# The second half of a weight transposition on ACT's DMA queue, the bias rows on SP's

## The chip, the cores and the metric

The kernel runs on one core of one Trainium2 chip. A core has five engines with a queue each: TensorE (PE, matmuls; its weight loads are listed apart as PEld), VectorE (DVE), ScalarE (ACT), GpSimd (POOL) and SyncE (SP). DMAs are issued in this kernel from the queues of SP and ACT; the names SPq and ACTq in the profile are these issues. The metric is the time of one execution in microseconds on the device, the median of the runs; lower is better.

## The reference

A layer norm of x (2048 tokens of 512 values, bf16), and then two branches on the normalised xn whose outputs are added to x.

```
xn = layernorm(x)
# branch A: linear attention, 32 heads of 16
q, k, v = split(xn @ wqkv)
pq, pk  = q @ w_phi, k @ w_phi                      # per head, 16 x 16
phi(p)  = concat(softmax(p), softmax(-p))           # 32 features per head
kv, z   = sum over tokens of phi(pk)^T v, of phi(pk)
o       = (phi(pq) @ kv) / (phi(pq) @ z + 1e-6)
# branch B: a dense layer with the mish activation, F = 1792
h       = xn @ w1 + b1
act     = h * tanh(softplus(h))
out     = x + o @ wo + act @ w2
```

## The kernel before, in words

The 2048 tokens are 16 tiles of 128 (NT), in four groups of four (NG, TPG). x stays in SBUF as `x_sb`; the normalised tiles are transposed into `xnT` and serve as weights of the projections and as moving operand of the dense layer.

*Keys' weights.* The keys' projection and w_phi are folded into one matrix `wkp` on the chip: `load_turned(D, 2)` (line 161) loads the keys' 512 columns of wqkv transposed, as tile `wT`, by two DMA transpositions (line 166) of 256 rows each, into columns 0 to 255 and 256 to 511. `fold` (line 171) multiplies one 128-column strip of wT by the block-diagonal `Wbd` (made by POOL from `wsrc` and `block`). So foldk_0 and foldk_1 need the first half of wT, foldk_2 and foldk_3 the second. The queries' weights are folded the same way much later (`load_turned(0)`, one transposition of all rows), and aren't touched by the change.

*The first DMAs (lines 548 to 559).* SP issues wsrc, then the two halves of wT, then wv, x's tiles 4 to 7, the two halves of w1, and x's tiles 8 to 15. ACT issues x's tile 0, x's tiles 1 to 3, and the bias rows `b1b` (14 x 128). ACT's first arithmetic is a square root of a constant (`root`, line 564), ahead of which the table of its functions is loaded; it has that table ready by the time the first row statistics come.

*Until the first tile is there*, PE runs 11 matmuls on constants (`keep_warm`, line 586).

*The order.* Behind the first DMAs all work follows a list written out by hand, `PLAN` (line 20), which `step` (line 593) turns into instructions; each engine runs its own in this order, and waits where an operand is missing. Its beginning is

```
spread_0 block mean_0 deviate_0_1 invert_0_1 total_3 spread_2 apply_0_0 scatter_3 mean_2 flip_0
spread_1 foldk_0 deviate_2_1 foldk_1 flip=_0_1 foldk=_0_0 invert_2_1 mean_1 foldk_2 deviate_3_1
```

spread and mean are the row statistics on DVE (lines 197, 213), deviate the square root of the variance on ACT (line 218), invert its reciprocal on DVE (line 223), apply the normalisation (line 249), total and scatter the statistics of tile 3 on ACT (lines 202, 206), flip the transposition of a normalised tile on PE (line 257), flip= its copy to SBUF (line 623), foldk a fold on PE (line 174), foldk= its copy into wkp (line 627), first a part of a keys' projection (line 274), bias the transposition of b1b on PE (line 633). Later steps project values, logits and the dense layer's units, take the softmaxes, and run the second half of the attention with the second dense layer (lines 524, 533).

Of the kernel before, what the change touches and what calls it, by code (L numbers as in the profile page):

```python
# [85 lines left out]
def kernel(  # L86
# [12 lines left out]
    nc = tc.nc  # L99
# [17 lines left out]
    b1_v = B_b1.rearrange("(f p) -> f p", p=P)  # L117
# [25 lines left out]
    b1b = wts.tile([FT, P], BF16, name="b1b")  # L143
# [17 lines left out]
    def load_turned(base_col, parts=1):  # L161

        wT = lnp.tile([P, 4, 512], BF16, name="wT", tag="xn")
        n = D // parts
        for r in range(0, D, n):
            nc.sync.dma_start_transpose(
                out=wT[:, :, r : r + n], in_=A_wqkv[r : r + n, base_col : base_col + D]
            )
        return wT
# [379 lines left out]
        nc.sync.dma_start(wsrc[:], wphi_v)  # L549
    for t in (slice(0, 1), slice(1, 4)):  # L550
        nc.scalar.dma_start(x_sb[:, t, :], x_v[:, t, :])
    nc.scalar.dma_start(b1b[:], b1_v[:, :])
    held = {"wT": load_turned(D, 2)}
    nc.sync.dma_start(wv, wqkv_v[:, :, 2 * D : 3 * D])
    nc.sync.dma_start(x_sb[:, 4:8, :], x_v[:, 4:8, :])
    for c in (slice(0, F // 2), slice(F // 2, F)):
# [36 lines left out]
    def step(name):  # L593
# [53 lines left out]
        elif kind == "wo":  # L647
            nc.sync.dma_start(wo_sb, wo_v[:, :, :])
        elif kind == "wq":
            held["wT"] = load_turned(0)  # L650
        elif kind == "fold":
            held[key] = fold(held["wT"], *n)
# [87 lines left out]
```

## Time and profile before

| what | value |
|---|---|
| median of 3 runs (lowest, highest) | 174.26 us (174.21, 174.62) |
| the profiled execution's own time | 174.22 us |
| its span, first to last instruction | 172.5 us |
| PE busy | 168.5 us (98%) |
| DVE, ACT, POOL busy | 150.6, 113.0, 49.5 us |
| DMA issues on ACT's queue before its first arithmetic | x_sb twice, 0.91 us together, then b1b, 0.73 us |
| transpositions of wT on SP's queue | from 1.31 us, 3.07 us for both issues |

Times in the profile are counted from the span's first instruction, so that a run takes some 1.7 us more than its span. A row of the timeline has the start, the length, the engine, the line in the kernel, the operation and the tiles, and in brackets the idle time of the engine ahead of it with what ended it. "Landing" of a DMA is when its last part has arrived and its semaphore tells so.

### The profile page before, as it was taken

The numbers are of one execution on the slowest core, as the hardware profiler recorded it, in microseconds if no ns is written. First come the engines' busy times: TensorE is split into PE (matmuls) and PEld (weight loads), VectorE is DVE, ScalarE is ACT, GpSimd is POOL, SyncE is SP. The second block draws the span as 40 slices with busy tenths as digits, with TensorE's granted clock in tenths as the row PEclk, the third lists the DMA queues.
The fourth block names the chain that finished last, engine by engine and source line by source line (L and its number), as shares of the span: only waits on it lengthen the run. The fifth ranks groups of instructions, "written<-read, shape, count | busy, mean of one in ns | idle before, by whom it ended". The sixth has DMA issues, their size and how long they took to land.

```text
span 172.5 us, 2832 instructions
## 1 busy us (share of the span) xinstructions
PE 168.5 (98%) x1038; PEld 82.6 (48%) x1038; DVE 150.6 (87%) x265; ACT 113.0 (66%) x169; POOL 49.5 (29%) x91
## 2 busy tenths in 40 slices
PE   8999999999999999999999999999999999999993
PEld 2444444444544644455454444544544554445571
DVE  2967998999999999999999999999999899994633
ACT  4949999999999799999999998821710400400000
POOL 6003047100480005685007403341480420320000
PEclk9999999999999999999999999999999999999999
DMA  6999992647900000000000095217456556676752
GB/s 154 264 397 347 130 331 89 128 117 143 104 0 0 4 0 0 2 0 4 0 0 0 0 131 117 61 37 163 47 121 138 130 130 93 143 164 152 124 143 71
DMA packets 45226, 18.03 MB, mean 105 GB/s; under 512 B 37148, under 2 KB 45212, under 8 KB 45212
## 3 DMA queue, kind: packets, MB, share of 16 engines
q1 hardware_dynamic: 44496, 17.26, 44.5%
q10 hardware_dynamic: 716, 0.59, 1.1%
q8 instruction: 8, 0.13, 0.3%
q14 instruction: 6, 0.05, 0.1%
HBM read 6.84 MB, written 2.10 MB: 52 GB/s over the span
## 4 chain that ended last, share of the span: by engine, by line
PE 94%; DVE 2%; DMA 1%; ACT 1%; issue 0%; DVEq 0%
PE ph L289 28%; PE po L524 28%; PE pproj L274 24%; PE po L533 8%; PE pnd L488 2%; PE pkv L451 2%; DMA x_sb<-in_A_x_dram 1%; DVE stats L197 1%; PE pfold L174 1%; DVE x_sb L541 1%; PE ptr L257 1%; DVE xn L249 0%; ACT wkv L627 0%; ACT rstd L218 0%; DVE rstd L223 0%
## 5 line engine op out<-in xcount | busy, mean ns | idle before, releaser
L524 PE MATMUL po<-w_sb,acts 128*128 128x512 bf16 (+1 forms) x238 | 51.9, 366 | 0.0
L289 PE MATMUL ph<-xnT,w_sb 128*128 128x512 bf16 x224 | 50.9, 379 | 0.0
L377 ACT ACTIVATE e<-e 128x1024 bf16<-128x1024 bf16 x28 | 28.3, 1056 | 25.1 <-DVE e L347 25.0
L391 POOL TENSOR_TENSOR t<-e 128x512 f32<-128x512 bf16 x13 | 16.6, 1274 | 78.2 <-ACT e L377 78.1
L299 ACT ACTIVATE acts<-ph,b1f 128x512 bf16<-128x512 f32 x56 | 35.4, 706 | 1.2 <-PE ph L289 1.1
L289 PEld LDWEIGHTS <-w_sb 128*128 128x128 bf16 x224 | 21.5, 98 | 25.2 <-issue 0.4
L524 PEld LDWEIGHTS <-acts 128*128 128x128 bf16 x238 | 22.5, 98 | 22.9
L274 PE MATMUL pproj<-wkv,xnT 128*128 128x512 bf16 x128 | 29.4, 379 | 0.0
L274 PEld LDWEIGHTS <-xnT 128*128 128x128 bf16 x192 | 18.0, 98 | 20.1 <-ACT xnT L623 0.3
L387 DVE TENSOR_REDUCE sums<-e 128x64 f32<-128x1024 bf16 x15 | 17.9, 1212 | 1.0 <-ACT e L377 0.8
L391 POOL TENSOR_TENSOR t<-t 128x256 f32<-128x256 f32 (+1 forms) x28 | 16.1, 576 | 2.2
L533 PE MATMUL po<-wqk,ob 128*128 128x512 bf16 (+1 forms) x68 | 16.3, 366 | 0.0
L274 PE MATMUL pproj<-wqk,xnT 128*128 128x512 bf16 x64 | 15.3, 379 | 0.0
L541 DVE TENSOR_TENSOR x_sb<-po,x_sb 128x512 bf16<-128x512 f32 (+1 forms) x17 | 10.9, 650 | 4.1 <-PE po L533 4.1
L197 DVE BATCH_NORM_STATS2 stats<-x_sb 128x6 f32<-128x512 bf16 x15 | 9.4, 679 | 4.1 <-DMA x_sb<-in_A_x_dram 4.1
L504 DVE TENSOR_TENSOR ob<-pnd,r 128x512 bf16<-128x512 f32 x16 | 11.1, 691 | 0.5
L438 DVE TENSOR_TENSOR e<-e,r 128x2048 bf16<-128x2048 bf16 x8 | 9.9, 1231 | 0.3
L326 ACT CAST e<-pproj 128x512 bf16<-128x512 f32 x12 | 7.1, 605 | 4.4 <-PE pproj L274 3.9
L533 PEld LDWEIGHTS <-ob 128*128 128x128 bf16 x68 | 6.4, 98 | 6.0
L503 DVE RECIPROCAL r<-pnd 128x32 f32<-128x32 f32 x16 | 5.6, 351 | 4.0 <-PE pnd L488 3.8
L309 ACT CAST p<-pproj 128x512 bf16<-128x512 f32 x14 | 7.8, 597 | 1.6 <-PE pproj L274 1.6
L488 PEld LDWEIGHTS <-qT 128*128 128x128 bf16 x128 | 6.1, 97 | 3.9 <-issue 0.9
(80 smaller groups left out, 184.6 us busy)
## 6 DMA issues: line engine op xcount, KB each, us to landing
out_dram<-x_sb SPq DMA_DIRECT2D x15, 128.0 KB, 1.9
w_sb<-in_B_w_dram SPq DMA_DIRECT2D x2, 896.0 KB, 8.4
x_sb<-in_A_x_dram SPq DMA_DIRECT2D x3, 512.0 KB, 10.2
w_sb<-in_B_w_dram SPq DMA_DIRECT2D x2, 640.0 KB, 5.5
wkv<-in_A_wqkv_dram SPq DMA_DIRECT2D x1, 512.0 KB, 5.1
w_sb<-in_B_w_dram SPq DMA_DIRECT2D x1, 512.0 KB, 7.0
wqk<-in_A_wo_dram SPq DMA_DIRECT2D x1, 512.0 KB, 4.2
x_sb<-in_A_x_dram ACTq DMA_DIRECT2D x1, 384.0 KB, 3.2
```

The source lines that it names most:

```text
L197: nc.vector.bn_stats(statistics(t)[0][:, t % TPG, :], x_sb[:, t, :])
L274: nc.tensor.matmul(pp, lhsT=xnT[:, t, kt, :], rhs=w[:, kt, :], start=(kt == 0), stop=(kt == KT - 1),)
L289: nc.tensor.matmul(ph[:], lhsT=w1_sb[:, kt, f * P : (f + 1) * P], rhs=xnT[:, g * TPG : (g + 1) * TPG, kt, :], start=(kt == 0), stop=(kt == ...
L299: nc.scalar.activation(acts[:, f, g * 512 : (g + 1) * 512], ph[:], ACT.Mish, bias=b1f[:, f : f + 1])
L377: nc.scalar.activation(v, v, ACT.Exp)
L387: nc.vector.reduce_sum(out, part, axis=AX.X)
L391: nc.gpsimd.tensor_tensor(out=to[:], in0=part[:, :, 0:n], in1=part[:, :, n : 2 * n], op=ALU.add)
L438: nc.vector.tensor_tensor(out=vv, in0=vv, in1=r2[:, :, None, :].to_broadcast([P, 128, 8, 2]), op=ALU.mult)
L504: nc.vector.tensor_tensor(out=o_t.rearrange("p (u v g d) -> p u v g d", u=2, v=4, g=4), in0=nd[:, :, :, 0:64].rearrange("p u v (g d) -> p ...
L524: nc.tensor.matmul(po[:, c], lhsT=acts[:, f, t * P : (t + 1) * P], rhs=w2_sb[:, f, c], start=(f == 0), stop=False,)
L533: nc.tensor.matmul(po[:, c], lhsT=oT_of[h][:, 2 + t % 2, j * P : (j + 1) * P], rhs=wo_sb[:, j, c], start=False, stop=(j == 3),)
L541: nc.vector.tensor_tensor(out=y, in0=po[:, c], in1=y, op=ALU.add)
```

## The change

The second half of the keys' wT is issued on ACT's queue, where it follows x's first two loads; the first half stays on SP. The bias rows' load leaves ACT's queue and is issued by SP behind the first half of wT, ahead of wv. The rest of SP's and ACT's orders, the order on PE, DVE and POOL, and the arithmetic are the same.

```
         wT = lnp.tile([P, 4, 512], BF16, name="wT", tag="xn")
         n = D // parts
         for r in range(0, D, n):
-            nc.sync.dma_start_transpose(
+            (nc.scalar if r and parts == 2 else nc.sync).dma_start_transpose(
                 out=wT[:, :, r : r + n], in_=A_wqkv[r : r + n, base_col : base_col + D]
             )
         return wT
...
     for t in (slice(0, 1), slice(1, 4)):
         nc.scalar.dma_start(x_sb[:, t, :], x_v[:, t, :])
-    nc.scalar.dma_start(b1b[:], b1_v[:, :])
     held = {"wT": load_turned(D, 2)}
+    nc.sync.dma_start(b1b[:], b1_v[:, :])
     nc.sync.dma_start(wv, wqkv_v[:, :, 2 * D : 3 * D])
     nc.sync.dma_start(x_sb[:, 4:8, :], x_v[:, 4:8, :])
```

More of the change, by code (lines that the diff above doesn't have):

```diff
@@ L165, in load_turned @@
         for r in range(0, D, n):
-            nc.sync.dma_start_transpose(
+            (nc.scalar if r and parts == 2 else nc.sync).dma_start_transpose(
                 out=wT[:, :, r : r + n], in_=A_wqkv[r : r + n, base_col : base_col + D]
@@ L551 @@
         nc.scalar.dma_start(x_sb[:, t, :], x_v[:, t, :])
-    nc.scalar.dma_start(b1b[:], b1_v[:, :])
     held = {"wT": load_turned(D, 2)}
+    nc.sync.dma_start(b1b[:], b1_v[:, :])
     nc.sync.dma_start(wv, wqkv_v[:, :, 2 * D : 3 * D])
```

## The prediction

> **What bounds the kernel now.** I read the page first (busy shares, then the chain that ended last), then the chain in order of time over the first 9 us, and then the queues of ACT and SP row by row.
>
> ```profile
> span 172.5 us, 2832 instructions
> PE 168.5 (98%) x1038; PEld 82.6 (48%) x1038; DVE 150.6 (87%) x265; ACT 113.0 (66%) x169; POOL 49.5 (29%) x91
> PE 94%; DVE 2%; DMA 1%; ACT 1%; issue 0%; DVEq 0%
> ```
>
> The chain is TensorE for 94% of the span. The next rows are the windows (length; PE busy and its matmuls; granted clock; DMA share; GB/s).
>
> ```profile
> 5.58:8.02 2.44, 2.34 (x30) 1.00 1.01 235
> 8.02:100.00 91.98, 91.98 (x553) 1.00 0.34 87
> 100.00:168.70 68.70, 68.70 (x444) 1.00 0.59 120
> ```
>
> From 8.02 us to 168.70 PE has no idle time at all. So a start delayed by some time is an end delayed by that time; and nothing behind 8 us can give it back. What sets that start is the head of the chain (start, us, what):
>
> ```profile
> 0.79 2.29 DMA x_sb<-in_A_x_dram
> 3.11 0.70 DVE stats L197
> 3.83 0.19 DVE mv L213
> 4.05 0.30 ACT rstd L218
> 4.38 0.16 DVE rstd L223
> 4.54 0.67 DVE stats L197
> 5.21 0.33 DVE xn L249
> 5.58 0.40 PE ptr L257 x4
> ```
>
> The first x tile lands at 3.08, and ACT's square root for it (deviate_0) at 4.05 stands in the middle of the chain. Whatever keeps ACT from it moves the whole kernel.
>
> **The change, part by part.** ACT's and SP's queues before (timeline):
>
> ```profile
> 0.79 0.91 ACTq L551 DMA_DIRECT2D x_sb<-in_A_x_dram  x2
> 1.73 0.73 ACTq L552 DMA_DIRECT2D b1b<-in_B_b_dram  x1
> 2.49 1.28 ACT L564 ACT_TABLE_LOAD   x1 [2.49 <-issue]
> 3.79 0.20 ACT L564 ACTIVATE root<-eps 128x1 f32<-128x1 f32 x1
> 1.31 1.32 SPq L166 DMA_TRANSPOSE wT<-in_A_wqkv_dram  x1
> 2.69 1.70 SPq L166 DMA_TRANSPOSE wT<-in_A_wqkv_dram  x1
> 4.43 0.58 SPq L554 DMA_DIRECT2D wkv<-in_A_wqkv_dram  x1
> ```
>
> The table load starts 0.03 us after the last DMA issue: ACT runs its DMA issues and its arithmetic in one order. ACT has almost no slack: root ends at 3.99, and deviate_0's statistics are ready at 4.02.
>
> (1) *The wait that the edit brings.* The built program of the changed kernel shows it (the text behind each is what the instruction waits for):
>
> ```
> ACT  L551 DMACopy x_sb_82<-in_A_x_dram 128x3x512
> ACT  L166 DmaTransposeAnt wT_108<-in_A_wqkv_dram 128x4x256 [waits DMAHW3_49]
> ACT  L564 LoadActFuncSet
> PE   L174 Ldweights wT_108 [waits DMAHW3_49]
> ```
>
> DMAHW3 is the semaphore that PE's first fold waits for: the landing of the first half of wT. So ACT may not issue the second half before the first has landed, and the table load, root and deviate_0 are queued behind that. In the kernel before, both halves are on SP without a wait. The landing of the first half (the DMA issue in the window 1.3 to 1.4; the last number is us from issue to landing):
>
> ```profile
> wT<-in_A_wqkv_dram SPq DMA_TRANSPOSE x1, 4.5
> DMA to landing us min/median/max: 3.8/4.1/4.5
> ```
>
> (The second row is the two halves together, so the second takes 3.8.) SP's rows ahead of the first half do not change: it is issued at 1.31 and lands at 1.31 + 4.5 = 5.81. ACT has been free since 1.70 and waits 4.1 us.
>
> (2) *The issue itself, on ACT.* 1.32 or 1.70 us by the two SP rows above. I take 1.32: like that one, it finds its own queue empty. ACT is free at 5.81 + 0.02 + 1.32 = 7.15, and at 7.53 by the other. The table load starts 0.03 later (7.18), and lasts 1.28, also beside full DMA traffic:
>
> ```profile
> 13.89 1.28 ACT L299 ACT_TABLE_LOAD   x1 [0.27 <-DVE b1f L635]
> ```
>
> Root follows at 7.18 + 1.30 = 8.48, ends at 8.68, and deviate_0 starts at 8.70, not 4.05: **4.65 us later** (5.03 with 1.70). Behind deviate_0 wait invert_0 and, in DVE's order, spread_2 and apply_0; on ACT total_3 and scatter_3. All move together, so flip_0 goes from 5.58 to 10.23.
>
> (3) *b1b goes to SP.* ACT saves 0.73, which lies wholly inside the new wait. On SP it costs 0.73 and the second half's 1.70 is gone: wv, x's tiles 4 to 7, w1 and the rest go out 1.0 us earlier. That is worth nothing: PE had no wait for them, and they now have 4.65 us more. b1b's reader (bias) is on PE at 12.44, 9 us after its new issue.
>
> (4) *The second half's own landing.* PE waited 0.19 us for it:
>
> ```profile
> 6.51 0.45 PEld L174 LDWEIGHTS <-wT 128*128 128x128 bf16 x8 [0.19 <-DMA wT<-in_A_wqkv_dram]
> ```
>
> In the new order it is issued at 5.83 and wanted at 6.32 + 4.65 = 10.97 at the earliest. With 3.8 or 4.5 it lands at 9.6 or 10.3: nothing. Wv, x and w1 are in flight beside it; bounded by the whole wT later in the trace, twice the rows in 5.9, it lands at 11.7, 0.8 late. I take 0 and keep 0.8 for the range.
>
> (5) *TensorE's clock.* The 11 matmuls that keep PE busy ahead of the first tile end at 5.42, and PE then idles until 10.23. How it runs at the start, and what it is granted at the very end, after the last matmul (169.6):
>
> ```profile
> 0.83 4.59 PE L584 MATMUL warm<-const-bfloat16-1.0 128*128 128x512 bf16 x11 [0.83 <-PEq L724]
> 0.83:5.00 4.17, 4.17 (x10) 1.00 0.85 204
> 13.58 6.91 PE ph L289 x32
> 59.70 0.67 PE pfold L174 x12
> 169.60:172.20 2.60, 0.00 (x0) 1.00 0.32 101
> 172.20:172.50 0.30, 0.00 (x0) 0.62 0.00 0
> ```
>
> A 512-column matmul takes 0.417 us at first (4.17 / 10) and 0.216 later (6.91 / 32): PE starts at half speed for 4.2 us (the profile's clock column does not show that one, but the pitch does). At the end the granted clock falls, 2.6 to 2.7 us after PE's last work. The hole here is 4.8 us, so I expect PE to restart at half speed. Its work from flip_0 to 8.02 is 28 matmuls of 128 columns (three flips of 4, four folds of 4) and one of 512: 28 x 0.056 + 0.216 = 1.78 us in a window of 2.44. At half speed it is 28 x 0.108 + 0.417 = 3.44, so the continuous part begins 1.0 later. If half speed lasts 4.2 us again, to 14.43, the 0.77 us left of it (from 13.66) lose half, 0.4. Together 1.4. The lower end is 0 (the clock stays up, rival A). For the upper, the 4.2 us count only from 12.8, when folds and second flip with their waits are through: half speed to 17.0, and 1.0 + (17.0 - 13.66) / 2 = 2.7. I take the middle value, because the row at the start is the nearest, and PE is then as busy as there.
>
> [...]
>
> **Sum**: 4.65 + 1.4 = 6.05 us. The profiled execution took 174.22 us (172.5 of span and 1.7 around it), 0.04 below the median of 174.26. 174.22 + 6.05 = 180.27; I say **180.2 us**, slower by 3.4%. About 0.3% is what a measurement of this kernel can tell from no change.
>
> [...]
>
> **Rivals.**
>
> *A: the same wait, but the clock stays up.* For it: the granted clock is 1.00 through 169.60:172.20, so 2.6 us idle is borne, and the moment at which it falls may depend on where PE's work lies. Against: the hole is nearly twice that. Time: 174.22 + 4.65 = 178.9; 178.5 if the first half, with no second half behind it on its queue, lands 0.4 earlier.
>
> *B: ACT does not stand at the wait, only issues later.* If the wait cost nothing, the second half would be issued at 1.73 for 1.32, the table load would start at 3.08 instead of 2.49, root end at 4.58 and deviate_0 start at 4.60: still 0.55 late, and 0.55 on the end, 174.8. Against: a queue with a wait does stand, as SP's with its later transpositions:
>
> ```profile
> SPq L264 <- DVE xn L249: 1.8, 1, 1.8
> ```
>
> *C, the other side: ACT only hands the transposition over, and neither its wait nor its issue holds the queue.* Then the table load stays at 2.49 and deviate_0 at 4.05, bound by DVE's statistics, and the second half starts at 1.73 instead of 2.69 and lands before PE wants it. The gain is at most PE's idle time in its head: 0.16 ahead of flip_0 and 0.10 in 5.58:8.02, so 174.0. It decides if ACT is free by 2.46 and the second half lands before 6.3. Against: the second half can't be under way before the first has landed at 5.81 if the wait is kept, and SP's own issues of this form last 1.32 and more where b1b's 0.73 lasted until 2.46.
>
> *D: the second half lands late.* If it shares the DMA engines with w1 for longer than the 5.9 row bounds, by 2 us more, PE waits at its third fold: 182.0.
>
> **How the numbers follow.** Forecast (wait and half speed) 0.70, A 0.20, D 0.06, B 0.02, C 0.02. The low end is A's 178.5; the high end is the forecast with the upper clock term, 4.65 + 2.7, 181.6, which also holds an issue of 1.70 (0.38 more) or a landing 0.8 late with the middle one. Below 178.5 stand B, C and a little of A, above 181.6 most of D. Slower by over 0.3% are the forecast, A, D and most of B (0.55 us is just past 0.3%): 0.97. C's 174.0 is within 0.3%: 0.02, and 0.01 is left for faster.
>
> **What the changed profile should show.** ACT's table load at about 7.2 (2.49 before), a wT issue on ACT's queue that starts near 5.8, deviate_0 at 8.7, flip_0 at 10.2, and PE idle from 5.42 to there. SP's wv at about 3.4. PE's folds with a pitch of 0.11, and 512-column matmuls of 0.42, up to about 14.4; the granted clock below 1.00 somewhere between 7.5 and 15. From there on the same PE stream without idle time, and the same tail. I am wrong if the first half of wT lands much earlier than 5.8, if the table load does not stand behind the wait, or if PE finds work that shortens the hole.

## The result and the profile after

The changed kernel takes 185.71 us (185.39 to 185.95), the kernel before 174.26: the ratio is 1.0647 (95% interval 1.0633 to 1.0662), 11.4 us slower. The forecast was 180.2, 6 us slower, with a range of 178.5 to 181.6: the sign is right, the size is about half.

The page of the changed kernel, its first rows, the granted clock in 40 slices (4.6 us each, tenths of full speed), and the chain's shares:

```profile
span 184.1 us, 2813 instructions
PE 169.8 (92%) x1021; PEld 84.3 (46%) x1038; DVE 150.8 (82%) x265; ACT 113.0 (61%) x169; POOL 49.5 (27%) x91
PEclk9855699999999999999999999999999999999999
PE 84%; DMA 8%; DVE 5%; issue 1%; SPq 0%; DVEq 0%
```

The span has grown by 11.6 us, all at the front: the clock is low in the second to the fifth slice, and a DMA now stands in the chain with 8% (14.7 us). (DVE's 5% are mostly a stretch from 120.6 to 129.5 us in which PE is busy too: 14.89 of the 15 us from 116 to 131.) The chain in order of time says which (start, us, what):

```profile
1.33 4.28 DMA wT<-in_A_wqkv_dram
5.63 10.37 DMA wT<-in_A_wqkv_dram
16.04 1.03 PE pfold L174 x8
17.07 0.43 PE ptr L257 x4
18.35 2.99 PE pproj L274 x7
25.23 6.91 PE ph L289 x32
180.33 1.02 DVE x_sb L541 x2
```

The first half of wT lands at 5.61, only then is the second issued, and it takes 10.4 us to land. Neither x nor ACT's arithmetic is in this chain. The first dense units start at 25.23 (13.58 before, 11.65 earlier), and the last residual at 180.33 (168.74 before, 11.59): next to nothing is lost or won behind the head.

ACT's queue and its first arithmetic (timeline), then all of PE's waits (in total, times, longest):

```profile
5.63 1.90 ACTq L166 DMA_TRANSPOSE wT<-in_A_wqkv_dram  x1
7.55 1.28 ACT L564 ACT_TABLE_LOAD   x1 [7.55 <-issue]
8.96 0.28 ACT L218 ACTIVATE rstd<-mv,eps 128x1 f32<-128x1 f32 x1
PE ptr L257 <- DVE xn L249: 5.4, 1, 5.4
PE pfold L174 <- DMA wT<-in_A_wqkv_dram: 4.2, 1, 4.2
```

The first wait, for the first tile, was forecast (10.39 for flip_0, 10.23 said). The second, for the second half of wT, was put at nothing. Why it lands so late is in the DMA queues between 12 and 13 us (packets, MB, share of the 16 engines; q1 is SP's queue with w1, q10 is ACT's with the second half):

```profile
q1 hardware_dynamic: 191, 0.34, 88.3%
q10 hardware_dynamic: 188, 0.05, 21.1%
```

As many packets of one as of the other. A packet of q10 is 256 bytes, and one of q1 is 1792 (0.34 MB / 191): by bytes the second half gets an eighth of the traffic. At 256 bytes the half has 1024 packets (0.26 MB), 64 for each of 16 engines on average; 16 engines x 1 us / 190 pairs is 84 ns for a pair, and 64 pairs take 5.4 us.

That is half of the 10.4 us. The queues from 5.63 us, when ACT issues the half, to 9.7 (first row), and from 9.7 to 15.4 (the other two):

```profile
q1 hardware_dynamic: 1222, 1.41, 101.3%
q1 hardware_dynamic: 1217, 1.81, 88.1%
q10 hardware_dynamic: 1054, 0.26, 21.1%
```

For 4.1 us no packet of the half moves; then all of its packets go, in 5.6 us, and the landing comes 0.6 us later. What the half waits for in the 4.1 us the profile doesn't show.

### The profile page after: what moved, and what is told of

Same layout as the page of the kernel before. It is cut to its first block, busy times and chain, and to the rows that moved or that the text cites. A ratio compares the mean times of both kernels' runs of the same rounds, so it can differ in the third digit from the quotient of the medians.

```text
span 184.1 us, 2813 instructions
## 1 busy us (share of the span) xinstructions
PE 169.8 (92%) x1021; PEld 84.3 (46%) x1038; DVE 150.8 (82%) x265; ACT 113.0 (61%) x169; POOL 49.5 (27%) x91
## 4 chain that ended last, share of the span: by engine, by line
PE 84%; DMA 8%; DVE 5%; issue 1%; SPq 0%; DVEq 0%
PE ph L289 26%; PE po L524 23%; PE pproj L274 23%; DMA wT<-in_A_wqkv_dram 8%; PE po L533 6%; PE pkv L451 2%; PE pnd L488 2%; DVE x_sb L541 1%; PE pfold L174 1%; DVE ob L504 1%; DVE m L340 1%; DVE e L347 1%; DVE sums L387 1%; PE ptr L257 1%; DVE r L503 0%
## 5 line engine op out<-in xcount | busy, mean ns | idle before, releaser
L524 PE MATMUL po<-w_sb,acts 128*128 128x512 bf16 (+1 forms) x232 | 51.1, 366 | 0.4
L391 POOL TENSOR_TENSOR t<-e 128x512 f32<-128x512 bf16 x13 | 16.6, 1274 | 79.6 <-ACT e L377 79.6
L274 PE MATMUL pproj<-wkv,xnT 128*128 128x512 bf16 x123 | 30.9, 396 | 0.3
L274 PEld LDWEIGHTS <-xnT 128*128 128x128 bf16 x192 | 18.5, 100 | 20.8 <-issue 1.4
L541 DVE TENSOR_TENSOR x_sb<-po,x_sb 128x512 bf16<-128x512 f32 (+1 forms) x17 | 10.9, 652 | 4.1 <-PE po L533 4.1
```

What stands on the lines that cost most here:

```text
L274: nc.tensor.matmul(pp, lhsT=xnT[:, t, kt, :], rhs=w[:, kt, :], start=(kt == 0), stop=(kt == KT - 1),)
L391: nc.gpsimd.tensor_tensor(out=to[:], in0=part[:, :, 0:n], in1=part[:, :, n : 2 * n], op=ALU.add)
L524: nc.tensor.matmul(po[:, c], lhsT=acts[:, f, t * P : (t + 1) * P], rhs=w2_sb[:, f, c], start=(f == 0), stop=False,)
L541: nc.vector.tensor_tensor(out=y, in0=po[:, c], in1=y, op=ALU.add)
```

## The experiments

Each experiment starts from the changed kernel; only the first is shown as an edit of the kernel before. Ratios are to the kernel before, run again on the same chip (174.30 to 174.40 us). The expectations call the cause tested "theory".

### Only the bias rows

```
     for t in (slice(0, 1), slice(1, 4)):
         nc.scalar.dma_start(x_sb[:, t, :], x_v[:, t, :])
-    nc.scalar.dma_start(b1b[:], b1_v[:, :])
     held = {"wT": load_turned(D, 2)}
+    nc.sync.dma_start(b1b[:], b1_v[:, :])
```

Here both halves stay on SP.

> Only the bias rows move to SP's queue (behind both halves of the transposition); both halves stay on SP, so there is no wait on ACT. If the move of the second half is the whole cause: ACT's table load starts at about 1.75 instead of 2.49, nothing else moves, 174.3 us within 0.3. If the bias rows on SP matter (everything behind them 0.7 us later): up to 174.9.

Measured: 174.28 us, ratio 0.9996 (0.9985 to 1.0006). The table load starts at 1.74, 0.75 us earlier, and deviate_0 at 4.19, still behind DVE's statistics. So moving the bias rows is worth nothing, and the whole loss belongs to the transposition's second half.

### SP's bulk loads held back

```
     nc.sync.dma_start(x_sb[:, 4:8, :], x_v[:, 4:8, :])
+    probe = consts.tile([P, 4, 1], BF16, name="probe")
+    nc.sync.dma_start(probe[:], held["wT"][:, :, 511:512])
     for c in (slice(0, F // 2), slice(F // 2, F)):
         nc.sync.dma_start(w1_sb[:, :, c], w1_v[:, :, c])
```

> The changed kernel, but SP issues w1 and x's last eight tiles only once the second half of wT has landed (a tiny DMA that reads wT stands ahead of them). Theory (the second half lands late because its small packets take turns with SP's bulk loads): it lands at 9.7 to 10.8 instead of 16.0, the third fold no longer waits, what is left is the 4.9 us of ACT's delay and some half-speed clock, 180 to 181 us. Rival (a transposition issued by ACT behind a wait is slow by itself): it lands near 16 again, 185.5 us.

Measured: 179.69 us, ratio 1.0299 (1.0266 to 1.0331), 6.0 less than the changed kernel and just below what was expected. The rows: ACT's issue, the landing of that half (us from issue), and PE's folds.

```profile
5.47 1.32 ACTq L166 DMA_TRANSPOSE wT<-in_A_wqkv_dram  x1
DMA to landing us min/median/max: 5.2/5.2/5.2
10.06 1.91 PE L174 MATMUL pfold<-Wbd,wT 128*128 128x128 bf16 x16
```

It lands at 10.7 and all 16 matmuls of the folds run in one piece. The issue on ACT takes 1.32 here and 1.90 in the changed kernel, where SP issues its loads at the same time (4.34 to 8.71 us; here SP has no issue from 4.29 to 10.74). So this transposition is not slow merely because ACT issues it: 5.2 us to landing here, 10.4 in the changed kernel. The queues from the issue, 5.47, to 7.8 us (first row) and from 7.8 to 10.2:

```profile
q1 hardware_dynamic: 769, 0.77, 101.0%
q10 hardware_dynamic: 1056, 0.26, 84.2%
q1 hardware_dynamic: 238, 0.23, 26.9%
```

So the half starts to move 2.4 us after its issue instead of 4.1, and needs 2.3 us instead of 5.6. Of the 5.2 us by which it lands sooner after its issue, 3.3 are in its transfer, where it takes turns, and 1.7 ahead of its first packet, where it doesn't. With the landing out of the way the chain goes through ACT, as the prediction had it (start, us, what):

```profile
5.47 1.32 ACTq L166
6.82 1.28 ACT L566
9.66 0.61 PE ptr L257 x4
```

TensorE still falls to half speed, for 6.83 us (length; PE busy; granted clock):

```profile
7.90:14.73 6.83, 5.07 (x33) 0.50 0.65 128
```

### TensorE kept busy

```
-spread_0 block mean_0 deviate_0_1 invert_0_1 total_3 spread_2 apply_0_0 scatter_3 mean_2 flip_0
+spread_0 block mean_0 deviate_0_1 invert_0_1 total_3 spread_2 apply_0_0 scatter_3 mean_2 (23 x warm) flip_0
...
-foldk_2
+(20 x warm) foldk_2
```

Each "warm" is one matmul on constants; in the kernel the word stands 23 and 20 times.

> The changed kernel with 23 more matmuls on constants ahead of flip_0 and 20 ahead of the third fold, so that PE stays busy in both holes. Theory (of the 11.4 us, 9.5 are the third fold's delay from 6.5 to 16.0 and 2 are half-speed clock): the granted clock stays 1.00, the third fold starts at 16.0 as before, 183.8 us. Rival (the clock costs nothing, because the head has slack): 185.7 us.

Measured: 183.51 us, ratio 1.0519 (1.0503 to 1.0534). The granted clock is 1.00 throughout, and the third fold still waits:

```profile
PEclk9999999999999999999999999999999999999999
16.21 0.62 PE L174 MATMUL pfold<-Wbd,wT 128*128 128x128 bf16 x8 [1.05 <-DMA wT<-in_A_wqkv_dram]
```

So the clock costs 185.71 - 183.51 = 2.2 us here. In the changed kernel it stood at one half for 13.65 us, behind 2.55 us in which PE had no work (length; PE busy; granted clock):

```profile
5.00:7.55 2.55, 0.00 (x0) 1.00 0.89 257
7.55:21.20 13.65, 6.62 (x37) 0.50 0.78 258
```

### ACT's arithmetic ahead of the wait

```
-    held = {"wT": load_turned(D, 2)}
+    held = {"wT": load_turned(D, 2, only=(0,))}
...
     nc.scalar.activation(root[:], eps[:], ACT.Sqrt)
+    load_turned(D, 2, held["wT"], (1,))
```

`load_turned` here issues only the halves named, into a tile that may be given.

> The changed kernel, with ACT's table load and root ahead of the transposition on its queue instead of behind it. They then run inside the wait, and deviate_0 starts at 7.5 instead of 9.0. Theory (the second half's landing sets the end): flip_0 comes 1.4 us earlier, the third fold still waits until 16.0, 185.7 us within 0.4. Rival (the prediction's: ACT's arithmetic held up behind the wait sets the end): 1.4 us less, 184.3 us.

Measured: 185.69 us, ratio 1.0637 (1.0612 to 1.0662), the changed kernel's time. deviate_0 starts at 7.51 and flip_0 at 8.96, both 1.4 us earlier, and PE waits longer for the fold instead (its waits):

```profile
PE pfold L177 <- DMA wT<-in_A_wqkv_dram: 5.8, 1, 5.8
PE ptr L260 <- DVE xn L252: 3.3, 1, 3.3
```

This takes away the prediction's main term as the cause: ACT is held up as was said, but in the changed kernel that isn't what the end waits for.

### No turn-taking and no slow clock

The held-back loads, with 23 matmuls on constants ahead of flip_0.

```
-... scatter_3 mean_2 flip_0
+... scatter_3 mean_2 (23 x warm) flip_0
```

> The held-back bulk loads (w1 and x's last eight tiles only once the second half of wT has landed) and 23 more matmuls on constants ahead of flip_0: neither turn-taking nor a slow clock is left, only the wait and the issue on ACT. Theory: flip_0 at 9.7 and the third fold at 10.6 to 10.7, 4.2 us later than before, 178.5 us; so the clock's part of the held-back kernel is 0.9 to 1.2. If the holding back itself costs (w1 late): above 179.5.

Measured: 179.48 us, ratio 1.0325 (1.0264 to 1.0385). This missed: the constants ran until 10.3, past the moment when the tile was ready, and flip_0 started at 10.31 right behind them. With 18 in place of 23:

> The held-back bulk loads with 18 constant matmuls ahead of flip_0 in place of 23, which had run past the moment at which flip_0 could start, by about half a microsecond. Theory: the clock stays at 1.00, flip_0 starts at 9.7 to 9.9 and waits for its tile, the third fold at 10.6 to 10.9, 178.7 to 179.0 us. If the rest of the miss of the 23-matmul version is the late bulk loads, it stays: 0.3 to 0.4 us beyond the head's 4.2.

Measured: 178.67 us, ratio 1.0246 (1.0225 to 1.0267). Now PE does wait for both, shortly (and once more, behind the head):

```profile
PE pfold L174 <- DMA wT<-in_A_wqkv_dram: 0.5, 1, 0.5
PE ptr L257 <- DVE xn L249: 0.3, 1, 0.3
PE pnd L488 <- DMA qT<-e: 0.2, 1, 0.2
17.71 6.91 PE ph L289 x32
```

The dense units start 4.1 us later than before (13.58), the time is 4.4 later than 174.30, the kernel before on the same chip. The 0.3 between them arises behind the head. The wait of 0.2 us at line 488, for a DMA into qT, is part of it: the profiles of the kernel before, of the changed kernel and of the first held-back one have no such wait. Whether it comes from the late bulk loads, and from which of them, was not tried.

### The same, with ACT's arithmetic ahead of the wait

With 18 constants ahead of flip_0 and 7 ahead of the third fold, and then with 12 and 7 (the loads of w1 and of x's last eight tiles move down to here from their place above):

```
-    held = {"wT": load_turned(D, 2)}
+    held = {"wT": load_turned(D, 2, only=(0,))}
...
     nc.scalar.activation(root[:], eps[:], ACT.Sqrt)
+    load_turned(D, 2, held["wT"], (1,))
+    probe = consts.tile([P, 4, 1], BF16, name="probe")
+    nc.sync.dma_start(probe[:], held["wT"][:, :, 511:512])
+    for c in (slice(0, F // 2), slice(F // 2, F)):
+        nc.sync.dma_start(w1_sb[:, :, c], w1_v[:, :, c])
+    for t in (8, 12):
+        nc.sync.dma_start(x_sb[:, t : t + 4, :], x_v[:, t : t + 4, :])
```

> As the kernel with held-back loads and more matmuls on constants, and with ACT's table load and root ahead of its transposition; 18 constant matmuls ahead of flip_0, 7 ahead of the third fold. Theory (first half's landing, then issue, then second half's landing: that chain sets the end even without turn-taking): flip_0 comes at 8.3, the third fold still at 10.7, 178.5 us. Rival (ACT's arithmetic behind the wait sets the end once the bulk loads are out of the way): 1.4 us less, 177.1 us.

Measured: 179.90 us, ratio 1.0332 (1.0300 to 1.0364). This one told nothing: the constants ran past both waits, and the third fold began at 11.59, when the half had landed at 10.9. (Its profiled execution, 181.0 us, is the slowest of its four, and has 1.8 us of the wait for qT.)

> The same with ACT's table load and root ahead of its transposition, and 12 constant matmuls ahead of flip_0 and 7 ahead of the third fold. Theory (the chain of two landings sets the end): flip_0 at 8.3 to 8.5, the third fold at 10.7 to 11.0 on the landing, the same time as the version with 18 within 0.4. Rival (ACT's arithmetic sets the end): 1.3 us less than that version.

Measured: 178.30 us, ratio 1.0228 (1.0203 to 1.0254). flip_0 starts at 8.49 (9.61 in the version with 18) and the third fold at 10.70 (10.98): 1.1 us earlier for ACT's arithmetic gives 0.4 of time, where the rival asked for 1.3. The run isn't clean: the half landed at 10.2 this time, and the fold came at 10.70 right behind the constants, so up to 0.5 more may have been there to gain. But a landing at 10.2 is itself 3.7 us after the third fold of before (6.5): even without turn-taking, the two landings one behind the other account for most of the delay. ACT's arithmetic comes out close behind them: it was worth 0.4, or 0.9 with the 0.5.

### Shorter packets for w1

```
-    for c in (slice(0, F // 2), slice(F // 2, F)):
+    for c in (slice(0, F // 4), slice(F // 4, F // 2), slice(F // 2, 3 * F // 4), slice(3 * F // 4, F)):
         nc.sync.dma_start(w1_sb[:, :, c], w1_v[:, :, c])
```

> The changed kernel with w1 loaded in four parts instead of two, so that its packets are 896 bytes long instead of 1792, the same bytes in all. Theory (the DMA engines take one packet of each queue in turn, whatever its size): about as many packets of both queues in each stretch, a pair takes 55 to 60 ns instead of 87, and the second half of wT lands at 13.6 to 14.4 instead of 16.0; 183.5 to 184.3 us. Rival (the queues share by bytes or by time): no earlier landing, 185.7 us.

Measured: 184.01 us, ratio 1.0568 (1.0542 to 1.0594). The queues between 12 and 13 us, and the third fold:

```profile
q1 hardware_dynamic: 309, 0.27, 78.9%
q10 hardware_dynamic: 307, 0.08, 34.5%
14.36 1.03 PE L174 MATMUL pfold<-Wbd,wT 128*128 128x128 bf16 x8 [2.74 <-DMA wT<-in_A_wqkv_dram]
```

Again one packet of each in turn, now 52 ns for a pair (16 engines x 1 us / 308 pairs). With half the packet length on the other queue the transposition lands at 14.3 and not at 16.0: its packets start at 9.7 us as in the changed kernel, and are through in 4.1 us in place of 5.6 (the queue from 9.7 to 13.8):

```profile
q10 hardware_dynamic: 1055, 0.26, 30.4%
```

In these two kernels the queues do not share by bytes or by time. (One part of this is not pure: SP's issues of x's last two loads run from 8.32 to 14.70 us here, past the half's landing at 14.3, and from 5.44 to 8.71 in the changed kernel; they stand behind the rest of the bulk.)

### Both halves on ACT, without the wait

```
-            (nc.scalar if r and parts == 2 else nc.sync).dma_start_transpose(
+            (nc.scalar if parts == 2 else nc.sync).dma_start_transpose(
```

> Both halves of wT on ACT's queue behind x's loads, one behind the other without a wait; the bias rows on SP as in the changed kernel. ACT is held only by the two issues, about 3 us, so deviate_0 starts at about 6.4 (4.05 before, 8.96 in the changed kernel). Theory (turn-taking with SP's loads makes the landing late, wait or not): the first half lands at 8 to 9.5, the second at 12 to 13.5, 181 to 183 us with some half-speed clock. Rival (the wait for the first half is what makes the landing late): the second half lands by 8.5, 176.5 to 177.5 us.

Measured: 185.44 us, ratio 1.0646 (1.0620 to 1.0671): as slow as the changed kernel, and slower than expected. The two issues take 4.98 us (1.30 and 3.65) and hold ACT nearly as long as the wait did; the halves land at 10.8 and 16.6 (issue, landing from issue):

```profile
1.74 4.98 ACTq L166 DMA_TRANSPOSE wT<-in_A_wqkv_dram  x2
wT<-in_A_wqkv_dram ACTq DMA_TRANSPOSE x1, 9.1
wT<-in_A_wqkv_dram ACTq DMA_TRANSPOSE x1, 13.5
```

No wait stands here between the halves, and the end is the same. The wait is thus not needed for this loss. How much of it is turn-taking this run doesn't say: the issues hold ACT, the clock falls too (0.963 in the mean), and between 5.2 and 6 us the queues moved 141 packets (SP) and 260 (ACT), not one of each; between 12 and 13 it is 192 and 188 again.

## Why the prediction was right in sign and wrong in size

The runs split the 11.4 us: 4.4 for the wait and the chain of two landings (held-back loads, constants: 178.67 against 174.30), 4.8 more for what SP's bulk loads do to the second half's landing (183.51 - 178.67) and 2.2 for the clock (185.71 - 183.51). The prediction had 4.65, 0 and 1.4. That 4.65 is so near to 4.4 is in part luck: it is the delay of ACT's arithmetic, and the second landing, which it put at nothing, happens to come at about the same time even with the bulk held back; the 4.4 also hold the 0.3 from behind the head.

- *The wait (1)*: right. The first half landed at 5.61 (5.81 forecast), and ACT, free since 1.71, issued the second at 5.63: 3.9 us of waiting.
- *The issue and ACT behind it (2)*: right as a sequence, mis-sized a little. The issue took 1.90, more than both rows it was bounded by (1.32, 1.70); the table load started at 7.55 (7.18), deviate_0 at 8.96 (8.70), flip_0 at 10.39 (10.23). But this was not what the end waited for: root ahead of the wait gave 1.4 us back at flip_0 and nothing at the end.
- *The bias rows (3)*: right, nothing.
- *The second half's landing (4)*: **the step that failed.** It was put at 0 and bounded at 0.8 late, by the whole wT later in the trace, twice the rows in 5.9 us. That transposition ran with no second queue at work. Here it landed at 16.0, 4.6 later than the third fold could have started (10.39 + 0.4 + 0.6 for flip_0 and the first eight matmuls at full rate). Of the larger time to landing, 10.4 against 5.2 us with the bulk held back, some 3.3 are turn-taking, as halving w1's packets bears out; 1.7 are a later first packet, and their cause stays open. An estimate of the transfer was to be had from before: 64 packets for each DMA engine at about 15 ns (507 to 575 in half a us from 4.5 to 5.5), each with one of w1's ahead of it at 70 ns (230 from 12 to 13), make 5.4 us. That the queues would alternate was not to be read there.
- *The clock (5)*: right that PE falls to half speed in the hole, mis-sized with (4). The granted clock fell to 0.50 at 7.55, 2.55 us after PE's last work, and came back at 21.20, not at 14.4, when PE had been busy again from 16.0 on; in the held-back kernel, which has no second hole, it came back at 14.73. The stretches at half speed were 13.65 and 6.83 us, one twice the other; that the 4.2 us from the start of the kernel before would come again was the author's estimate, and what sets the length is not shown. It cost 2.2 us instead of 1.4. With the third fold on time it cost about 1.0 (179.69 - 178.67, where the first has an interval of 0.6 to either side).
- *The rivals*: A was refuted in the profiled execution, where the clock stood at 0.50 for 13.65 us (two of the five runs, 185.46 and 185.39 us, have a mean clock of 1.00 on record, the other three 0.963). B's price, 174.8, was wrong by more than 10 us by the kernel with no wait, though that one moves both halves. C did not occur: ACT stood from 1.71 to 5.63. D had the right mechanism, a late landing from sharing with w1, with 0.06 of the chances and 2 us for what was 4.8.

## What to carry to other kernels

When a transfer is moved to another DMA queue, ask what it will take turns with: beside SP's bulk the half got here only one packet of 256 bytes for each of 1792 (188 and 191 in 1 us). Size it by packets, its packets for each engine times the time of a pair (64 times 84 ns here, 5.4 us of the 5.6 measured), and not by a row without a second queue; and add the time until its first packet, which was 4.1 us here and 2.4 with the bulk held back. The DMA that had to wait on ACT held the arithmetic behind it, here the table load, at 7.55 in place of 2.49; but look for the landing at the end of that wait too, since here that was the later of the two (16.0 against 10.39 for flip_0).

## What was not expected of the hardware

Two queues shared the 16 DMA engines one packet each, at 256 against 1792 bytes (188 and 191 in 1 us) as at 256 against 896 (307 and 309). It isn't so everywhere: in the kernel before, SP's queue moved 359 packets, most of them of w_phi (0.01 MB in all), and ACT's 112 (of x) between 2.5 and 3.0 us. A transposition that had 3.8 us to landing ahead of the bulk on its own queue took 10.4 beside it. The issue of a transposition on ACT's queue took 1.32 us with the bulk held back, 1.90 while SP issued the bulk, and 3.65 for the second of two in a row; what makes it longer was not tried.
